# Feature weights of a Hedgehog attention kernel: two loads replaced by one load and a copy made by TensorE

## The chip, the cores and the metric

The kernel runs on one core of one Trainium2 chip. The metric is the time of one execution in device microseconds. The engines are TensorE (PE in the profile, with its weight loads as PEld), VectorE (DVE), ScalarE (ACT), GpSimd (POOL) and SyncE (SP, which here only issues DMAs).

## What is computed

Attention with a feature map instead of a softmax over keys, followed by a gated linear unit with a causal convolution of five taps, for 8 batches of 8 heads, 576 rows and 64 columns. Cut to what matters:

```
def phi(x):                                  # w_phi is 64 x 128
    proj = x @ w_phi
    proj = proj - max(|proj|, axis=-1)
    return concat([exp(proj), exp(-proj)])
q_p, k_p = phi(q), phi(k)
kv  = sum over s of k_p[s, f] * v[s, d]
z   = sum over s of k_p[s, f]
x   = (q_p @ kv) / (q_p @ z + 1e-6)          # heads side by side: 8 x 576 x 512
gate = sigmoid(causal 5-tap convolution of x with conv_w)
out  = (gate * (x @ w_val)) @ w_out
```

The weights `w_phi` are one 64 x 128 array of 32 KB, the same for q and k and for all heads and batches.

## The kernel before, in words

Each batch is laid out with two rows or two heads side by side: 64 columns of the one in partitions 0 to 63, of the other in partitions 64 to 127 (`par` 0 and 1 in the code). After a transpose, `XT_["k"]` and `XT_["q"]` (kT and qT in the profile) hold the inputs with the 64 columns over the partitions, in 18 blocks of 128 columns, worked on in five units (`UNITS`: 4, 4, 4, 4 and 2 blocks). For each block, `proj` (L570 to L578) runs two matmuls, one for each half of the partitions: the data stand in rows 0 to 63 or 64 to 127, and so the feature weights are needed in both halves too. That tile is `W2`, 128 x 128 in bf16, twice the same 64 rows. `qp` (L687) uses W2 the other way round, as the stationary operand.

`W2` is made in `c_w` (L451): ScalarE's queue issues two DMAs of `w_phi` into the two halves of `W32` (128 x 128, fp32), VectorE casts `W32` to `W2`, and ScalarE's queue then issues the load of the convolution weights `cw5`. (In the profile, buffer numbers are left out of names: W32 and W2 both appear as W.)

The first batch comes in by chunks: SyncE's queue issues four loads of K (`lk`, 288 KB each) and five of Q (`lq`, four of 256 KB and one of 128 KB) with `load32` (L520 to L527). They land in the memory of the second KTIL buffer, which is free at that time, so the profile shows them as KTIL. TensorE transposes them in fp32 (`tp32`, L536), and ScalarE or VectorE copies the result to bf16 (`tc32`, L542 and L544). Then come for each unit the K matmuls with W2 (`kp`), the row maxima on VectorE (`amax`, L585) and two exponentials on ScalarE (`kexp`, L595), and for Q the same with other steps between (`qm`, `mqt`, `rx`, `qp`, `qexp`). GpSimd waits for the last Q chunk (`hold`, L509) and then starts the loads of the next batches.

The order of the work is written out by hand. `build` makes a list of tasks, each with an index, an engine (or a choice of engines, settled by one letter of `FLEX`), and for tasks that write PSUM a group with one or two of the eight banks (digits of `BANKS`). `ORDER` lists the indices in the order in which the instructions are emitted; each engine runs its own instructions in that order. Durations and dependences given in `build` are notes for whoever made the order; the waits in the program follow from the tiles that are written and read. `WARM` and `ZERO` name positions in `ORDER` at which extra matmuls on constants are put in. A new task at the front of the list thus shifts every later index by one, and a new entry in `ORDER` every later position.

At the head, `ORDER` begins "1 2 9 3 4 11 5 6 10 21 22 19 20 13 12 46 ...": load K chunk 0, transpose K unit 0 (four transposes, bank 0), load K chunk 1, transpose K unit 1 (bank 3), load K chunk 2, copy unit 0 out, load Q chunks 1 and 0, transpose K unit 2 (bank 7), copy unit 1 out, K matmuls of unit 1, and so on. K unit 2 is the first that needs K chunk 2.

Of the kernel before, what the change touches and what calls it, by code (L numbers as in the profile page):

```python
# [17 lines left out]
F = 128  # L18
# [13 lines left out]
XH = R // 2  # L32
HALO = 16
XW = HALO + XH
WARM = (
    "60:6:1 81:1:1 87:7:2 134:7:1 141:7:1 "
)
ZERO = "35:76:7 61:80:5 75:34:1 101:105:1 118:99:1 126:215:8 144:223:1 155:192:4 158:200:1 175:315:6 189:346:1 195:241:2 197:241:2 211:327:1"
STD = 1.18
E1 = D + 1  # L40
QW = 2 * NR

ORDER = (
# [36 lines left out]
)  # L80
FLEX = (
    "AAAAAADAAADDPPPPDDDDAADDDDDDDDDDDDDAAADAAAADDDDAAADDDAADAAADDADAADDDDADDDDADDDDDDAADADDAAAAAA"
)
BANKS = (
    "037362307001454523232323016701676714232367230101676012354423010145454501013660564675601456745010145450101676767014501454"
    "545672012376701230167676745677773567232367232345452301672323232367674545015452343623670101232345454452230145450167676767"
    "010123014501230167450120167364012345236745454555723014545234567232323010123236745230167232346701422010167454567010121656"
    "701456701012301670123010167232367674567023677260123230123230167464644501016701670123676745672345232345450123670157672345"
    "010167452326322345670145670101674545012345012367452345010127452301014545670101765"
)  # L90


# [70 lines left out]
def build(plan, em=None):  # L163
# [16 lines left out]
    for b in range(B):  # L180

        if b == 0:
            last = A("lk", 0, 9, "SP", 0.3, None, rank=-1100)
            for w in "kq":
                lds = []
                for u in range(4 if w == "k" else NU):
                    pr = -1000.0 + (0 if w == "k" else 10) + u
                    last = A("l" + w, b, u, "SP", 0.65, fn("load32", w, u), [], rank=pr, lat=0.1)
                    lds.append(A("l" + w, b, u, "DMA", 0.9 if w == "k" else 0.2 * UNITS[u][1], None, [last], rank=pr))
                if w == "q":  # L190
                    hold = [None, A("lk", b, 0, "POOL", 0.15, fn("hold", HOLDU), [lds[HOLDU]], rank=-600)]
                for u, (c0, n) in enumerate(UNITS):
                    need = [lds[u]] if w == "q" else sorted(set(lds[J // 9] for J in (2 * c0, 2 * (c0 + n) - 1)), key=lambda t: t.idx)
                    pr = -900 + (0 if w == "k" else 50) + u
                    g = plan.group("tp", 1)
                    tp = A("kp", b, u, "PE", 0.22 * n, fn("tp32", w, u), need, g, 0, rank=pr)
                    h["x" + w, b, u] = A("kmax", b, u, ("DVE", "ACT"), (dve(n * P), act(n * P)), fn("tc32", w, u), [tp], g, rank=pr)
                    h["tp", w, u] = tp
# [62 lines left out]

        for u, (c0, n) in enumerate(UNITS):
            g = plan.group("kp", 2)
            kp = h["kp", b, u] = A("kp", b, u, "PE", 0.057 * n, fn("kp", b, u), [G("xk", b, u)], g, 1)
            h["kmax", b, u] = A("kmax", b, u, "DVE", dve(2 * n * P, 0.08), fn("kmax", b, u), [kp, G("ek", b - 2)], g)
            for s in range(2):
                h["kexp", b, u, s] = A("kexp", b, u, "ACT", act(2 * n * P), fn("kexp", b, u, s),
# [22 lines left out]

        for u, (c0, n) in enumerate(UNITS):
            g = plan.group("qm", 2)
            qm = h["qm", b, u] = A("qm", b, u, "PE", 0.057 * n, fn("qm", b, u), [G("xq", b, u)], g, 1)
            h["qmax", b, u] = A("qmax", b, u, "DVE", dve(2 * n * P, 0.08), fn("qmax", b, u), [qm, G("mqt", b - 2)], g)
        for i, us in enumerate(parts(b)):
            gm = plan.group("mqt", 1 if b == 0 else 2)
# [68 lines left out]
class Emit:  # L365
    def __init__(self, nc, tc, ctx, q, k, v, w_phi, moe_w_val, moe_conv_w, moe_w_out, out):
# [50 lines left out]
        ident = self.ident = T("ident", [P, P])  # L417
        nc.vector.tensor_copy(ident[:, :], ident_f[:, :])

        self.W32 = T("W32", [P, F], FP32)  # L420
        self.W2 = T("W2", [P, F])
        self.wphi = w_phi

# [26 lines left out]

    def c_w(self):  # L451
        nc = self.nc
        for i in range(2):
            nc.scalar.dma_start(self.W32[i * D:(i + 1) * D, :], self.wphi[:, :])
        nc.vector.tensor_copy(self.W2[:, :], self.W32[:, :])
        nc.scalar.dma_start(self.cw5[:, :], self.wts[1][:, :])

    def c_wv(self, t):
        self.nc.gpsimd.dma_start(self.WV[:, :, 0:DM], self.wts[0].rearrange("(i p) o -> p i o", p=P))
# [441 lines left out]
```

## Time and profile before

| what | value |
|---|---|
| median of three timed runs | 218.77 us (218.7, 218.77, 219.3) |
| span of the profiled execution, first to last instruction | 217.7 us |
| TensorE busy | 195.5 us, 90% of the span |
| ScalarE busy | 180.8 us, 83% |
| VectorE busy | 170.2 us, 78% |
| GpSimd busy | 132.8 us, 61% |
| data moved by DMA | 39.92 MB, 183 GB/s on the mean |

The profiled execution's own time is its span; what lies around the span is not in the trace. In lines of the profile, the name left of the arrow is written and the names right of it are read; the bracket at the end tells how long the engine had been idle and what ended that. In the chain of waits each line is a start, a duration and what was running or being waited for.

### The profile page before, as it was taken

What the parts mean: (1) busy time and instruction counts of PE and PEld (TensorE: products, weight loads), DVE (VectorE), ACT (ScalarE), POOL (GpSimd) and SP (SyncE); (2) the same over time, 40 slices, a digit from 0 to 9 for tenths busy, and PEclk for the clock granted to TensorE, in tenths of its full rate; (3) what the DMA queues carried; (4) which work ended last, traced back from release to release, by engine and by line L of the source; (5) the groups of instructions that cost most, each with busy time, mean ns of one, the idle gap of its engine ahead of it and who ended that gap; (6) DMA issues with size and microseconds to landing.
All of it is one profiled execution on the core that took longest, in us unless ns stands there. A gap on an engine that the chain in (4) does not pass through costs nothing.

```text
span 217.7 us, 9029 instructions
## 1 busy us (share of the span) xinstructions
PE 195.5 (90%) x3946; PEld 138.6 (64%) x3946; DVE 170.2 (78%) x257; ACT 180.8 (83%) x267; POOL 132.8 (61%) x172
## 2 busy tenths in 40 slices
PE   2787887778999999998999999999999999899990
PEld 2555565566676676676857776567757766687740
DVE  3199979999789988997899978998699897654510
ACT  3589999999989899998999997999988988634251
POOL 3055999897793838970999089902993879210010
PEclk9999999999999999999999999999999999999997
DMA  6999998899899799989999778969953265764166
GB/s 177 364 234 215 302 188 231 149 174 199 144 152 284 139 135 213 302 154 174 233 276 168 88 165 248 190 142 203 287 183 89 63 160 128 81 168 97 48 186 202
DMA packets 49954, 39.92 MB, mean 183 GB/s; under 512 B 34165, under 2 KB 39541, under 8 KB 49914
## 3 DMA queue, kind: packets, MB, share of 16 engines
q1 hardware_dynamic: 43616, 28.65, 55.6%
q0 software_dynamic: 6032, 10.49, 26.3%
q8 instruction: 31, 0.51, 0.9%
q10 hardware_dynamic: 266, 0.21, 0.3%
q14 instruction: 9, 0.07, 0.1%
HBM read 30.48 MB, written 9.44 MB: 183 GB/s over the span
## 4 chain that ended last, share of the span: by engine, by line
PE 52%; ACT 23%; DVE 14%; DMA 5%; issue 4%; SPq 0%; DVEq 0%; ACTq 0%
PE PS L791 11%; ACT QTIL L706 9%; PE PS L781 9%; PE PS L813 9%; ACT KTIL L595 8%; DVE MQP L585 5%; PE PS L620 5%; PE PS L577 4%; PE PS L719 4%; DVE MK L585 3%; DMA KTIL<-in_k_dram 3%; PE PS L693 2%; DMA XT<-XN 2%; PE PS L817 2%; PE PS L698 2%
## 5 line engine op out<-in xcount | busy, mean ns | idle before, releaser
L595 ACT ACTIVATE KTIL<-PS 128x1024 bf16<-128x1024 f32 (+1 forms) x80 | 71.9, 960 | 4.1 <-PE PS L577 2.0
L610 POOL TENSOR_TENSOR VT<-VN,EK 128x1152 bf16<-128x1152 f32 x32 | 67.9, 2123 | 4.0 <-ACT EK L604 3.9
L706 ACT ACTIVATE QTIL<-PS 128x1024 bf16<-128x1024 f32 x64 | 62.5, 1044 | 2.4 <-PE PS L698 1.6
L682 POOL TENSOR_TENSOR RX<-MQR,ident 128x512 bf16<-128x512 bf16 (+1 forms) x39 | 36.6, 964 | 35.7 <-DVE MQR L670 26.0
L585 DVE TENSOR_REDUCE MK<-PS 128x8 f32<-128x1024 f32 (+1 forms) x40 | 44.2, 1112 | 2.9 <-PE PS L577 1.2
L585 DVE TENSOR_REDUCE MQP<-PS 128x8 bf16<-128x1024 f32 (+1 forms) x40 | 43.6, 1112 | 3.1 <-PE PS L577 2.3
L791 PE MATMUL PS<-XT,WV 128*128 128x288 bf16 x256 | 34.8, 286 | 0.3 <-DVE GV L797 0.2
L797 DVE SCALAR_TENSOR_TENSOR GV<-TH,PS 128x576 bf16<-128x576 bf16 x32 | 23.8, 752 | 10.4 <-PE PS L791 4.7
L813 PE MATMUL PS<-WOUT,GV 128*128 128x512 bf16 x128 | 31.3, 380 | 0.0
L791 PEld LDWEIGHTS <-WV 128*128 128x128 bf16 x256 | 23.8, 98 | 7.9 <-issue 1.4
L785 ACT ACTIVATE TH<-PS 128x576 bf16<-128x576 f32 x32 | 20.3, 663 | 9.5 <-PE PS L781 6.3
L620 PE MATMUL PS<-VT,KTIL 64*128 64x65 bf16 x1152 | 23.3, 191 | 1.1 <-issue 1.0
L781 PE MATMUL PS<-XT,GW 64*64 64x288 bf16 x640 | 23.1, 285 | 0.9 <-DMA XT<-XN 0.8
L740 DVE TENSOR_TENSOR XN<-PS,RCP 128x512 bf16<-128x512 f32 x32 | 22.1, 692 | 1.5 <-DMA XT<-XN 0.4
L620 PEld LDWEIGHTS <-KTIL 64*128 64x128 bf16 x1152 | 20.8, 94 | 3.8 <-issue 2.5
L719 PEld LDWEIGHTS <-QTIL 128*128 128x128 bf16 x512 | 18.3, 97 | 6.4 <-issue 4.0
L719 PE MATMUL PS<-KV,QTIL 128*128 128x65 bf16 x512 | 20.3, 194 | 0.3 <-DVE MQP L585 0.2
L781 PEld LDWEIGHTS <-GW 64*64 64x64 bf16 x640 | 17.8, 106 | 3.3 <-DVE RCP L737 0.9
L634 ACT ACTIVATE OUTS<-PS 128x512 f32<-128x512 f32 x22 | 13.5, 619 | 7.3 <-PE PS L813 6.1
L577 PE MATMUL PS<-W,qT 64*128 64x128 bf16 x288 | 15.1, 217 | 3.7 <-ACT qT L544 0.9
L813 PEld LDWEIGHTS <-GV 128*128 128x128 bf16 x128 | 11.1, 98 | 11.3 <-issue 0.6
L577 PEld LDWEIGHTS <-qT 64*128 64x128 bf16 x288 | 10.6, 94 | 10.3 <-issue 5.2
(79 smaller groups left out, 235.6 us busy)
## 6 DMA issues: line engine op xcount, KB each, us to landing
out_dram<-OUTS SPq DMA_DIRECT2D x32, 256.0 KB, 3.4
VN<-in_v_dram SPq DMA_DIRECT2D x7, 1152.0 KB, 6.3
KQN<-in_q_dram POOLq DMA_DIRECT2D x6, 576.0 KB, 8.3
KQN<-in_k_dram POOLq DMA_DIRECT2D x6, 576.0 KB, 9.8
KTIL<-in_k_dram SPq DMA_DIRECT2D x4, 288.0 KB, 4.5
VN<-in_v_dram POOLq DMA_DIRECT2D x1, 1152.0 KB, 10.6
KTIL<-in_q_dram SPq DMA_DIRECT2D x4, 256.0 KB, 5.7
out_dram<-OUTS SPq DMA_DIRECT2D x14, 64.0 KB, 2.6
```

Of the source, the lines that this page charges most:

```text
L577: nc.tensor.matmul(self.PS[:, t.grp.banks[par], i * P:(i + 1) * P], X[rows, (c0 + i) * P:(c0 + i + 1) * P], self.W2[rows, :], start=True, ...
L585: self.nc.vector.tensor_reduce(o, self.two(t.grp, n * P).rearrange("p a (c f) -> p a c f", f=F), AX.X, ALU.max, apply_absolute_value=True)
L595: self.nc.scalar.activation(self.KTIL[b % 2][:, s, c0:c0 + n, :, :].rearrange("p c a f -> p a c f"), self.two(t.grp, n * P).rearrange("p a ...
L610: nc.gpsimd.tensor_tensor(self.VT[g][:, s, :, 0:D], self.VN[b % 2][:, NC * g:NC * g + NC, :], e.to_broadcast([P, NC, D]), ALU.mult)
L620: nc.tensor.matmul(self.PS[:, t.grp.banks[ab], (s * 2 + x) * E1:(s * 2 + x + 1) * E1], self.KTIL[b % 2][rows, s, J // 2, J % 2, :], self.V ...
L682: self.nc.gpsimd.tensor_tensor(o, *wide(self.MQR[self.mq(b, u)][:, :], self.ident2), ALU.mult)
L706: self.nc.scalar.activation(o, i, AF.Exp, scale=1.0 - 2.0 * s)
L719: nc.tensor.matmul(self.PS[:, t.grp.banks[h // 4], (h % 4) * E1:(h % 4 + 1) * E1], Q[:, s, c % 2, h, (c // 2) * P:(c // 2 + 1) * P], self. ...
L781: self.nc.tensor.matmul(self.PS[o * D:(o + 1) * D, t.grp.banks[par], 0:R], self.GW[r, jj, 4 - m, :], X[r, 4 * a + jj, :, HALO - 8 * s:HALO ...
L791: self.nc.tensor.matmul(self.PS[:, t.grp.banks[par], 0:R], self.WV[:, i, (2 * j + par) * D:(2 * j + par + 2) * D], X[:, 4 * par + i, :, HA ...
L797: nc.vector.scalar_tensor_tensor(out=self.GV[b % 3][:, j, :, :], in0=self.TH[j][:, :, :], scalar=1.0, in1=self.two(t.grp, R), op0=ALU.add, ...
L813: nc.tensor.matmul(self.PS[:, t.grp.banks[0], :], GV[:, j, c % 2, (c // 2) * XH:(c // 2) * XH + P], self.WOUT[:, j, c % 2, :], start=(j == ...
```

## The change

`w_phi` is loaded once, into a `W32` of 64 partitions, and cast by VectorE into a new bf16 tile `WB` of 64 partitions. Two new tasks stand at the front of the list. `c_wd`: TensorE multiplies a 64 x 64 identity with `WB`, twice, once into partitions 0 to 63 and once into partitions 64 to 127 of PSUM bank 7. `c_wd2`: VectorE copies the 128 x 128 result from PSUM into `W2`. A product with an identity in bf16 gives the bf16 values back, so W2 holds the same numbers as before. In `ORDER` the two stand behind the transposes of K unit 0 and ahead of the load of K chunk 1 and the transposes of K unit 1. All other entries of `ORDER` are in the same sequence, each index larger by two (index 0 stays); `FLEX` has one letter more at the front (D, for VectorE), `BANKS` one digit (7), and the positions and indices in `WARM` and `ZERO` are larger by two.

```
 ORDER = (
-    "1 2 9 3 4 11 5 6 10 21 22 19 20 13 12 46 25 26 7 8 23 24 14 27 28 42 29 ...
+    "3 4 11 1 2 5 6 13 7 8 12 23 24 21 22 15 14 48 27 28 9 10 25 26 16 29 30 44 31 ...
...
         if b == 0:
             last = A("lk", 0, 9, "SP", 0.3, None, rank=-1100)
+            g = plan.group("mqt", 1)
+            wd = A("mqt", 0, 0, "PE", 0.1, fn("c_wd"), [], g, 3, rank=-950)
+            h["w2",] = A("mqt", 0, 0, ("DVE", "ACT"), (dve(128), act(128)), fn("c_wd2"), [wd], g, rank=-950)
...
-        self.W32 = T("W32", [P, F], FP32)
+        self.W32 = T("W32", [D, F], FP32)
+        self.WB = T("WB", [D, F])
         self.W2 = T("W2", [P, F])
...
     def c_w(self):
         nc = self.nc
-        for i in range(2):
-            nc.scalar.dma_start(self.W32[i * D:(i + 1) * D, :], self.wphi[:, :])
-        nc.vector.tensor_copy(self.W2[:, :], self.W32[:, :])
+        nc.scalar.dma_start(self.W32[:, :], self.wphi[:, :])
+        nc.vector.tensor_copy(self.WB[:, :], self.W32[:, :])
         nc.scalar.dma_start(self.cw5[:, :], self.wts[1][:, :])
+
+    def c_wd(self, t):
+        for a in range(2):
+            self.nc.tensor.matmul(self.PS[a * D:(a + 1) * D, t.grp.banks[0], 0:F],
+                                  self.ident[0:D, 0:D], self.WB[:, :], start=True, stop=True)
+
+    def c_wd2(self, t):
+        self.ev(t, self.W2[:, :], self.PS[:, t.grp.banks[0], 0:F])
```

The first instructions of `kp` and `qm` for batch 0 also name the new copy as a dependence in `build`.

More of the change, by code (lines that the diff above doesn't have):

```diff
@@ L34 @@
 XW = HALO + XH
[L35 to L38, printed above, removed]
+WARM = "62:6:1 83:1:1 89:7:2 136:7:1 143:7:1"
+ZERO = "37:78:7 63:82:5 77:36:1 103:107:1 120:101:1 128:217:8 146:225:1 157:194:4 160:202:1 177:317:6 191:348:1 197:243:2 199:243:2 213:329:1"
 STD = 1.18
@@ L43 @@
 ORDER = (
[36 rows of a table removed]
[36 rows of a table added]
 )
 FLEX = (
-    "AAAAAADAAADDPPPPDDDDAADDDDDDDDDDDDDAAADAAAADDDDAAADDDAADAAADDADAADDDDADDDDADDDDDDAADADDAAAAAA"
+    "DAAAAAADAAADDPPPPDDDDAADDDDDDDDDDDDDAAADAAAADDDDAAADDDAADAAADDADAADDDDADDDDADDDDDDAADADDAAAAAA"
 )
 BANKS = (
[L85 to L89, printed above, removed]
+    "703736230700145452323232301670167671423236723010167601235442301014545450101366056467560145674501014545010167676701450145"
+    "454567201237670123016767674567777356723236723234545230167232323236767454501545234362367010123234545445223014545016767676"
+    "701012301450123016745012016736401234523674545455572301454523456723232301012323674523016723234670142201016745456701012165"
+    "670145670101230167012301016723236767456702367726012323012323016746464450101670167012367674567234523234545012367015767234"
+    "5010167452326322345670145670101674545012345012367452345010127452301014545670101765"
 )
@@ L263, in build @@
             g = plan.group("kp", 2)
-            kp = h["kp", b, u] = A("kp", b, u, "PE", 0.057 * n, fn("kp", b, u), [G("xk", b, u)], g, 1)
+            kp = h["kp", b, u] = A("kp", b, u, "PE", 0.057 * n, fn("kp", b, u), [G("xk", b, u), G("w2") if b == 0 else None], g, 1)
             h["kmax", b, u] = A("kmax", b, u, "DVE", dve(2 * n * P, 0.08), fn("kmax", b, u), [kp, G("ek", b - 2)], g)
@@ L292, in build @@
             g = plan.group("qm", 2)
-            qm = h["qm", b, u] = A("qm", b, u, "PE", 0.057 * n, fn("qm", b, u), [G("xq", b, u)], g, 1)
+            qm = h["qm", b, u] = A("qm", b, u, "PE", 0.057 * n, fn("qm", b, u), [G("xq", b, u), G("w2") if b == 0 else None], g, 1)
             h["qmax", b, u] = A("qmax", b, u, "DVE", dve(2 * n * P, 0.08), fn("qmax", b, u), [qm, G("mqt", b - 2)], g)
@@ L452, in c_w @@
         nc = self.nc
-        for i in range(2):
-            nc.scalar.dma_start(self.W32[i * D:(i + 1) * D, :], self.wphi[:, :])
-        nc.vector.tensor_copy(self.W2[:, :], self.W32[:, :])
+        nc.scalar.dma_start(self.W32[:, :], self.wphi[:, :])
+        nc.vector.tensor_copy(self.WB[:, :], self.W32[:, :])
         nc.scalar.dma_start(self.cw5[:, :], self.wts[1][:, :])
+    def c_wd(self, t):
+        for a in range(2):
+            self.nc.tensor.matmul(self.PS[a * D:(a + 1) * D, t.grp.banks[0], 0:F], self.ident[0:D, 0:D], self.WB[:, :], start=True, stop=True)
+    def c_wd2(self, t):
+        self.ev(t, self.W2[:, :], self.PS[:, t.grp.banks[0], 0:F])
     def c_wv(self, t):
```

72 rows, old and new, of the table ORDER are left out of this document.

## The prediction

> **What bounds the kernel now.** I read the page first, for the shares over the whole run, because the change touches only the first ten microseconds and I need to know whether a saving there is still there at the end.
>
> ```profile
> span 217.7 us, 9029 instructions
> PE 195.5 (90%) x3946; PEld 138.6 (64%) x3946; DVE 170.2 (78%) x257; ACT 180.8 (83%) x267; POOL 132.8 (61%) x172
> PE 52%; ACT 23%; DVE 14%; DMA 5%; issue 4%; SPq 0%; DVEq 0%; ACTq 0%
> ```
>
> No engine is free and none is full. The last row is the chain of waits that ended last: it hops between TensorE, ScalarE and VectorE, and only 5% of it is DMA. Every engine works through a written order, so a saving at the head of the chain can travel to the end, unless some other chain was nearly as late. So I read the chain in order of time for the head alone.
>
> ```profile
> 1.22 0.42 SPq L527
> 1.63 0.04 issue
> 1.67 5.58 DMA KTIL<-in_k_dram
> 7.25 0.04 issue
> 7.29 0.90 PE PS L536 x3
> 8.20 0.97 PE PS L577 x16
> 9.17 1.06 PE PS L536 x4
> ...
> 10.32 0.69 DVE qT L542
> 11.01 1.14 DVE MK L585
> ```
>
> The reader is to see that the third K chunk (issued at 1.67, landed at 7.25) is what the head waits for: three transposes of it, the first sixteen feature matmuls, four transposes of Q, and from 10.32 on VectorE and ScalarE hand on to each other. The feature weights W2, which the change is about, are not in the chain. So the question is what the change does to the landing at 7.25 and to TensorE between 3.85 and 10.3. That is the timeline's business, here by queue and engine (the row at 3.97 is the last of the three in the row above it):
>
> ```profile
> 0.73 1.23 ACTq L454 DMA_DIRECT2D W<-in_w_phi_dram  x2
> 0.74 1.37 SPq L527 DMA_DIRECT2D KTIL<-in_k_dram  x3
> 2.15 2.15 SPq L525 DMA_DIRECT2D KTIL<-in_q_dram  x3
> 3.97 0.33 SPq L525 DMA_DIRECT2D KTIL<-in_q_dram  x1
> 3.85 2.23 PE L536 MATMUL PS<-ident_f,KTIL 128*128 128x128 f32 x9 [3.85 <-DMA KTIL<-in_k_dram]
> 7.29 0.90 PE L536 MATMUL PS<-ident_f,KTIL 128*128 128x128 f32 x3 [1.21 <-DMA KTIL<-in_k_dram]
> 8.13 1.04 PE L577 MATMUL PS<-W,kT 64*128 64x128 bf16 x16
> ...
> 11.07 0.40 PE L577 MATMUL PS<-W,qT 64*128 64x128 bf16 x8 [0.19 <-DVE qT L542]
> ...
> 20.95 0.61 PE L555 MATMUL PS<-ident,QTIL 128*128 128x128 bf16 x8
> 5.29 0.23 DVE L455 CAST W<-W 128x128 bf16<-128x128 f32 x1 [2.48 <-DMA W<-in_w_phi_dram]
> 10.32 0.69 DVE L542 CAST qT<-PS 128x512 bf16<-128x512 f32 x1 [4.80 <-ACT KTIL L595]
> ...
> 16.69 0.21 DVE L667 TENSOR_SCALAR MQR<-PS 128x128 bf16<-128x128 bf16 x1
> 11.01 0.19 POOL L509 CAST HOLD<-KTIL 128x1 bf16<-128x1 f32 x1 [8.62 <-DMA KTIL<-in_q_dram]
> ```
>
> Three covers show. TensorE ends its first nine transposes at 6.08 and stands idle for 1.21 us until the third K chunk. W2 is cast by 5.52 and first used at 8.13, so it has 2.6 us in hand. VectorE is idle for 4.80 us before 10.32. Next the DMAs at the head, by issue with its time to landing (the first four rows are K chunks 0, 1 and 2 and the second W copy), with the two waits of SyncE's queue, the share of the ScalarE queue between 1.70 and 7.25, and the DMA share (next-to-last column, then GB/s) in two stretches.
>
> ```profile
> KTIL<-in_k_dram SPq DMA_DIRECT2D x1, 288.0 KB, 3.0
> KTIL<-in_k_dram SPq DMA_DIRECT2D x1, 288.0 KB, 3.5
> KTIL<-in_k_dram SPq DMA_DIRECT2D x1, 288.0 KB, 5.6
> W<-in_w_phi_dram ACTq DMA_DIRECT2D x1, 32.0 KB, 3.8
> KTIL<-in_q_dram SPq DMA_DIRECT2D x1, 256.0 KB, 5.7
> SPq L525 <- DMA W<-in_w_phi_dram: 1.2, 2, 0.8
> q10 hardware_dynamic: 170, 0.08, 4.8%
> 2.70:3.70 1.00, 0.00 (x0) 0.00 (x0) 0.11 (x2) 0.94 (x1) 0.00 (x0) 1.00 1.05 392
> 4.20:4.70 0.50, 0.50 (x4) 0.34 (x2) 0.00 (x0) 0.00 (x0) 0.00 (x0) 1.00 0.72 201
> ```
>
> Chunk 0 lands at 0.74 + 3.0 = 3.7, chunk 1 at 1.22 + 3.5 = 4.7, chunk 2 at 7.25, the second W copy at 1.35 + 3.8 = 5.15 (its issue is the second half of the 1.23 us row). At 2.70 to 3.70 the engines are full (share 1.05, 392 GB/s); at 4.20 to 4.70 there is a dip to 201 GB/s in the middle of chunk 2's flight. The first W copy has no landing time in the trace, but the Q issue at 3.97 is one of the two that waited for W, so that copy had landed by about 3.95.
>
> **The change part by part.** *One W copy fewer.* ScalarE issues one W load instead of two, and the conv weights behind it go out about 0.6 us earlier, which nothing in the head reads. What the lost copy takes from the DMA engines ahead of chunk 2 I bound from two rows. From below: ScalarE's queue, two W copies and the conv weights, took 4.8% of 16 engines over 5.55 us, which is 0.27 us of each engine; one copy is under half of it, 0.12. From above: 288 KB is 0.295 MB, at 392 GB/s 0.75 us, but chunk 1 landed 1.0 us after chunk 0, with the first W copy between them; if all of the excess is that copy, it costs 0.25. Less than nothing is also possible: where engines idle anyway, as in the dip, the copy's packets cost 0. I take 0.2, between the two rows and near the upper one, because the landing is what the path sees. Chunk 2 then lands at about 7.05, and that comes off the chain.
>
> The Trainium skill, "DMA: Bandwidth & Descriptors", Rules for kernel authors, says that two transfers to disjoint partition halves serialize on the same engines and that one should be used instead. The rows agree so far as the copies take engine time one after the other; by the 436 GB/s of its Anatomy section the copy's 32 KB would be an estimated 0.08 us, which would give 218.7 instead of 218.6.
>
> *SyncE's queue.* The two Q issues that waited for W (1.2 us together, 0.8 the longer) read no W. I take this to be a completion counter that an earlier DMA still holds, each issue reusing the counter of one a fixed number before it. With one DMA fewer at the front, the Q issue at 3.97 goes out up to 0.8 us earlier and those behind it 0.4 to 0.8. It buys nothing on the path: they queue behind chunk 2 and the first two Q chunks (the first of these lands at 2.15 + 5.7 = 7.85, and its transposes start at 9.17, 1.3 us later). The last Q chunk releases POOL at 11.01, which then loads the next batch; that may start 0.2 to 0.4 us earlier, and TensorE first touches the next batch at 20.95.
>
> *The cast.* 64 rows instead of 128, 0.23 us by the row, at about 4.05 instead of 5.29, since it waits for the first copy only: done by 4.3.
>
> *Two matmuls on TensorE, between the first four transposes and the next five.* By the nine in 2.23 us, 0.23 us each, the first four are issued by about 4.75, so the cast at 4.3 is not waited for. Sixteen W matmuls in 1.04 us run in pairs, 0.13 us a pair; the two new ones share their rows of the array, so I count a pair's time for each: 0.26 us. The next five transposes end at 6.34 instead of 6.08, and still 0.7 us ahead of 7.05: cost nothing, cover the wait for chunk 2. If that cover goes, 0.26 us goes onto the chain. Queued behind the new wait are all of TensorE's later transposes; who waits for those is ScalarE's copies, which have the same slack.
>
> *The copy out of PSUM on VectorE.* 128x128 from PSUM: the nearest row is 0.21 us (L667). It runs at about 5.4 to 5.6, inside VectorE's 4.80 us of idle time; W2 is ready at 5.6 instead of 5.52, needed at 7.9. It uses PSUM bank 7, which the third transpose group writes next; the group's first transpose may be held to 5.6, behind which it stands anyway. Cost nothing.
>
> The sum: 217.7 of span less 0.2 is 217.5. The three timed runs have a median of 218.77, 1.07 above the profiled span, and I take that difference as unchanged: 217.5 + 1.07 = 218.57, so 218.6. About 0.3%, or 0.66 us, is what a measurement of this kernel can tell from no change (its own runs spread from 218.7 to 219.3), so the forecast is "no difference that shows". From 10.3 us on I assume that the whole 0.2 travels. If another chain takes over, less does: 218.8. With the two bounds and half a run's spread, its own range is 218.3 to 219.0.
>
> **The rivals.** *The dip goes with the copy.* Chunk 2 lands 2.55 us after chunk 1 where 0.75 would do. If the small packets from ScalarE's queue cause that hold-up, chunk 2 lands a microsecond or more earlier. TensorE then becomes the bound at 6.34 (five transposes behind the new pair), and the gain is 7.25 - 6.34, or 0.9: 217.9. For it: the dip falls in the W copies' flight. Against it: one W copy flew beside chunk 1, which came in at nearly full rate.
>
> *The weights come late.* TensorE's queue is in order, so a late W load now holds all K transposes, where it formerly held only the first W matmuls at 8.13. It decides if W lands after about 5.4: then 0.1 + 0.23 for the cast, 0.26 for the pair and five transposes at 0.23 reach beyond 7.1, and each further microsecond is lost one for one. At 6.4 it is 1.0 us: 219.8. Against it: the first copy had landed by 3.95 and even the second at 5.15.
>
> *The TensorE clock turns earlier.* The matmuls tell of it: W matmuls run sixteen in 1.04 us at 8.13 and eight in 0.40 at 11.07.
>
> ```profile
> L536 PE MATMUL PS<-ident_f,KTIL 128*128 128x128 f32 x16 | 4.2, 433 | 5.1 <-DMA KTIL<-in_k_dram 5.1
> L536 PE MATMUL PS<-ident_f,KTIL 128*128 128x128 f32 x19 | 3.3, 295 | 0.3 <-DVE MQP L585 0.3
> ```
>
> The same transposes take 433 ns on the mean before 10 us and 295 after 10.6, although the granted clock of the windows reads 1.00 in both. If the two new matmuls shorten the idle time enough to bring the turn forward to 7.3, the 2.9 us of TensorE work in the chain from 7.29 to 10.2 shrinks by the ratio of the means, to 2.0: 0.9 us, plus the 0.2: 217.7. The Trainium skill, "TensorE: Matmul & The Clock Gate", Part 1, says that the clock rises after a busy window of about 3.4 us which runs free of the kernel; the same rule would let an unlucky phase delay the turn as easily, and no row of one execution can show either. Against it: 0.26 us of work in a 1.21 us hole leaves most of the hole.
>
> *The change brings nothing*: the copy's packets filled time in which the engines waited, and chunk 2 lands at 7.25 as before: 218.8.
>
> **How the numbers follow.** Forecast 0.60, nothing at all 0.16, dip gone 0.13, clock earlier 0.04, weights late 0.07. The predicted time is the forecast's, 218.6. The range runs from 217.8, which takes in the dip gone, to 219.1, which takes in the spread of no gain at all and leaves out the late weights. Faster by over 0.3% means under 218.11: dip and clock, 0.17, and 0.02 of the forecast's lower tail. Slower by over 0.3% means above 219.43: late weights, 0.07. The same: 0.74.
>
> **What would show it.** Right: one W row on ScalarE's queue; the cast before 4.75; two small matmuls between the fourth and fifth transpose; the five transposes done by 6.4 and then idle time ended by the third K chunk at 7.0 to 7.2; the chain of waits still opening with that chunk. Wrong: idle time on TensorE ended by the cast or by W; the third K chunk at 6.3 or earlier, or later than 7.4; transposes at 295 ns before 10 us; a span outside 216.7 to 218.0.

## The result, and the profile after

The kernel after takes 217.94 us in the median of 22 runs, the kernel before 218.8 us in 22 runs beside them. The ratio is 0.994 with a 95% interval of 0.9918 to 0.9961: faster, by 0.4 to 0.8%. Ratios leave out executions in a slower state of the chip and the medians do not, so the two medians are only 0.86 us apart where the ratio says 1.3. The forecast was 218.6 and "no difference that shows"; the range began at 217.8, so it held the median, but the direction was called wrong.

The page of the kernel after, in the same three rows as before:

```profile
span 215.2 us, 9031 instructions
PE 195.4 (91%) x3948; PEld 138.4 (64%) x3948; DVE 170.0 (79%) x258; ACT 180.5 (84%) x267; POOL 132.9 (62%) x172
PE 55%; ACT 22%; DVE 15%; issue 4%; DMA 1%; DVEq 0%; ACTq 0%
```

The engines' work is the same; the DMA share of the chain of waits fell from 5% to 1%. Of that, the K chunks went from 3% to 1%; the other 2% (a transfer named XT<-XN, later in the run) is missing from a second profile of the kernel before too (below, "before, twice"), so it is not the change's. The chain's head tells where the K chunks' part went (start, duration, what):

```profile
0.74 2.93 DMA KTIL<-in_k_dram
3.66 0.14 issue
3.80 1.09 PE PS L544 x4
4.89 0.24 PE PS L461 x2
5.13 1.90 PE PS L544 x8
7.03 0.97 PE PS L585 x16
8.00 0.71 PE PS L544 x4
...
8.80 0.69 DVE qT L550
```

The chain no longer waits for the third K chunk. After the first chunk TensorE runs through without a pause: four transposes, the two new doubling matmuls, eight transposes, the W matmuls. VectorE's first Q copy starts at 8.80 instead of 10.32, 1.52 us earlier. The timeline has the parts of the change (queues, TensorE, VectorE):

```profile
0.73 0.58 ACTq L455 DMA_DIRECT2D W<-in_w_phi_dram  x1
2.14 1.38 SPq L533 DMA_DIRECT2D KTIL<-in_q_dram  x3
4.82 0.31 PE L461 MATMUL PS<-WB,ident 64*64 64x128 bf16 x2
5.06 1.97 PE L544 MATMUL PS<-ident_f,KTIL 128*128 128x128 f32 x8
6.96 1.04 PE L585 MATMUL PS<-W,kT 64*128 64x128 bf16 x16
3.98 0.22 DVE L456 CAST WB<-W 64x128 bf16<-64x128 f32 x1 [1.58 <-DMA W<-in_w_phi_dram]
5.17 0.29 DVE L636 CAST W<-PS 128x128 bf16<-128x128 f32 x1 [0.97 <-PE PS L461]
```

And the landing of the third K chunk, issued at 1.67, stands in the DMA issues (the last number is the time from issue to landing):

```profile
KTIL<-in_k_dram SPq DMA_DIRECT2D x1, 288.0 KB, 4.1
```

It takes 4.1 us instead of 5.6: it lands at 5.81, while TensorE is still on the second unit's transposes. The W matmuls start at 6.96 instead of 8.13 (1.17 us), and from there to the Q copy it takes 1.84 us instead of 2.19 (0.35 us), because the last four transposes of the chain ran in 0.71 us instead of 1.06: the clock had turned. (By that is meant here that TensorE works slowly at first and from some moment on faster: the sixteen W matmuls take 1.04 us in both kernels, and 0.62 in those below that are warmed up.)

The two profiled spans differ by 2.5 us, the medians by 0.9. The head makes 1.52 us of the 2.5. The rest, 1.0 us, is about the length of a pause that nothing in the profile releases. The chain of the kernel before has it at 98 us:

```profile
98.03 0.96 issue
```

A second profile of the same kernel (below, "before, twice") has it at half the length,

```profile
98.23 0.47 issue
```

and the profile of after has none there. A second profile of after (e16 below), however, has two:

```profile
91.36 0.83 issue
96.85 0.70 issue
```

So these pauses vary between executions of one kernel and are not the change's; what makes them is not shown.

One more thing is earlier in after: GpSimd's wait for the last Q chunk ends at 9.95 us instead of 11.01, and its loads of the next batches with it. That this is not the source of the gain is told by the warmed kernel of before (e7 below), which gains as much with that wait ending at 10.68:

```profile
9.95 0.19 POOL L517 CAST HOLD<-KTIL 128x1 bf16<-128x1 f32 x1 [7.41 <-DMA KTIL<-in_q_dram]
10.68 0.19 POOL L509 CAST HOLD<-KTIL 128x1 bf16<-128x1 f32 x1 [8.29 <-DMA KTIL<-in_q_dram]
```

### The profile page after: what moved, and what is told of

Its sections match the earlier page's. It is cut to its first block, busy times and chain, and to the rows that moved or that the text cites. A ratio compares the mean times of both kernels' runs of the same rounds, so it can differ in the third digit from the quotient of the medians.

```text
span 215.2 us, 9031 instructions
## 1 busy us (share of the span) xinstructions
PE 195.4 (91%) x3948; PEld 138.4 (64%) x3948; DVE 170.0 (79%) x258; ACT 180.5 (84%) x267; POOL 132.9 (62%) x172
## 4 chain that ended last, share of the span: by engine, by line
PE 55%; ACT 22%; DVE 15%; issue 4%; DMA 1%; DVEq 0%; ACTq 0%
PE PS L799 11%; PE PS L821 10%; PE PS L789 9%; ACT QTIL L714 9%; ACT KTIL L603 9%; DVE MQP L593 5%; PE PS L727 5%; PE PS L585 4%; PE PS L628 4%; DVE MK L593 4%; PE PS L701 2%; PE PS L825 2%; PE PS L706 2%; PE PS L544 2%; DVE XN L748 2%
## 5 line engine op out<-in xcount | busy, mean ns | idle before, releaser
L789 PE MATMUL PS<-XT,GW 64*64 64x288 bf16 x640 | 23.6, 285 | 0.9 <-DVE RCP L745 0.4
```

What stands on the lines that cost most here:

```text
L789: self.nc.tensor.matmul(self.PS[o * D:(o + 1) * D, t.grp.banks[par], 0:R], self.GW[r, jj, 4 - m, :], X[r, 4 * a + jj, :, HALO - 8 * s:HALO ...
```

## The experiments

Three theories at first. A: the second copy's own rows, ahead of the third K chunk, hold that chunk up. B: the conv weights do, which the change moves ahead of the chunk. C: the landing varies by itself, and the gain has another source. Later D: a share of the gain is TensorE's clock.

**The copy put back, idle (e1, e15).** The kernel after, and the second load again, into a tile that nothing reads:

```
+        nc.scalar.dma_start(self.WX[:, :], self.wphi[:, :])      # behind the load of W32, [D, F] fp32
```

> The kernel after, with a second load of the feature weights put back in its old place on ScalarE's queue, into a tile that nothing reads. Theory A (the second copy's own packets and its place ahead of the third K chunk hold that chunk up): the third K chunk lands at 6.8 to 7.3 us as before and the time is 218.6 to 219.0, no better than the kernel before. Theory B (the conv weights do it: the change moves them ahead of that chunk): the same here, since the idle copy pushes them back too. Theory C (the landing varies by itself from one execution to the next, and the gain has another source): the time stays near 217.9.

The ratio to before is 1.0003 (0.9971 to 1.0036). TensorE's timeline of this kernel:

```profile
4.90 0.31 PE L463 MATMUL PS<-WB,ident 64*64 64x128 bf16 x2
5.15 1.33 PE L546 MATMUL PS<-ident_f,KTIL 128*128 128x128 f32 x5
6.86 0.90 PE L546 MATMUL PS<-ident_f,KTIL 128*128 128x128 f32 x3 [0.38 <-DMA KTIL<-in_k_dram]
7.69 1.03 PE L587 MATMUL PS<-W,kT 64*128 64x128 bf16 x16
```

The wait for the third chunk is back (landing at 6.81), and the whole gain is gone, though TensorE still doubles the weights. Theory C falls, and the doubling by itself brings nothing. Once more, on another occasion:

> The kernel with the idle second copy of the feature weights once more, on the same chip as the two with other sources: 6.4 to 7.2 us for the third K chunk and the time of before, by all theories.

1.004 (1.000 to 1.008), landing at 7.02.

**The copy behind the chunk (e2).** The kernel before, with no work added to TensorE:

```
-        for i in range(2):
-            nc.scalar.dma_start(self.W32[i * D:(i + 1) * D, :], self.wphi[:, :])
-        nc.vector.tensor_copy(self.W2[:, :], self.W32[:, :])
+        nc.scalar.dma_start(self.W32[0:D, :], self.wphi[:, :])
...
+            if u == 2:                                            # in load32, behind K chunk 2
+                self.nc.sync.dma_start(self.W32[D:P, :], self.wphi[:, :])
+                self.nc.vector.tensor_copy(self.W2[:, :], self.W32[:, :])
```

> The kernel before, with the second copy of the feature weights issued by SyncE's queue right behind the third K chunk, so that the conv weights go out second on ScalarE's queue; nothing is added on TensorE. Theories A and B: the third K chunk lands at 5.8 to 6.1 us, and without the 0.24 us of the two new matmuls the time is 217.6 to 217.9, at least as good as after. Theory C: 218.8, as before.

0.991 (0.9875 to 0.9946), landing at 5.50. Its timeline on TensorE:

```profile
3.90 2.79 PE L537 MATMUL PS<-ident_f,KTIL 128*128 128x128 f32 x12 [3.90 <-DMA KTIL<-in_k_dram]
6.63 1.03 PE L578 MATMUL PS<-W,kT 64*128 64x128 bf16 x16
7.59 1.35 PE L537 MATMUL PS<-ident_f,KTIL 128*128 128x128 f32 x8
```

All twelve K transposes run in one piece. The gain is had without the doubling and without one DMA fewer: what counts is that the copy is not ahead of the chunk.

**The conv weights late (e3), and before, twice (e4).** The kernel before with the conv weights issued by SyncE behind the last Q chunk; and the kernel before, unchanged.

```
-        nc.scalar.dma_start(self.cw5[:, :], self.wts[1][:, :])
+            if u == 4:                                            # in load32, behind Q chunk 4
+                self.nc.sync.dma_start(self.cw5[:, :], self.wts[1][:, :])
```

> The kernel before, both weight copies in place, with the conv weights moved from ScalarE's queue to SyncE's, behind the last Q chunk. Theory A: the third K chunk still lands at 6.8 to 7.3 us and the time stays 218.6 to 219.0. Theory B: it lands at 5.8 to 6.1 us and the time is 217.7 to 218.0. Theory C: 218.8, landing anywhere.

> The kernel before, unchanged, timed and profiled once more. Theories A and B: the third K chunk lands at 6.8 to 7.3 us again and TensorE's clock turns at its own moment. Theory C: the landing differs by half a microsecond or more from the 7.25 us of the first profile. Time 218.8 by all.

e3: 0.9969 (0.9935 to 1.0002), landing at 6.41, between the two expectations and unclear in time. e4: 0.9994 (0.997 to 1.0017), landing at 6.83. So the landing does vary from one execution to the next, as C said (by 0.4 us here, and by 1.1 between the two profiles of one kernel below, e10 and e14), but around a later moment than in after.

**One row, two copies, the copy last (e5, e6, e11).** The kernel after with idle loads of other sizes and places on ScalarE's queue:

```
+        nc.scalar.dma_start(self.WX[0:1, :], self.wphi[0:1, :])   # e5: one row, behind W32
+        nc.scalar.dma_start(self.WX[:, 0, :], self.wphi[:, :])    # e6: two copies, behind W32
+        nc.scalar.dma_start(self.WX[:, 1, :], self.wphi[:, :])
+        nc.scalar.dma_start(self.WX[:, :], self.wphi[:, :])       # e11: one copy, behind the conv weights
```

> The kernel after with an idle extra load in the old place of the second copy, but of one row of 512 bytes instead of 64 rows. Theory A1 (what holds the third K chunk up is the rows of the extra load, spread over all DMA engines): it lands near 5.8 us, as in after. Theory A2 (it is the extra load as such, its issue and completion, whatever its size, and the conv weights pushed behind the chunk): it lands at 6.4 to 7.2 us, as with the full idle copy.

> The kernel after with two idle extra loads of the feature weights instead of one, between the weights and the conv weights on ScalarE's queue. Theory A1 (rows) and A2 (each load): the third K chunk lands later still than with one (6.81 us), at 7.2 to 7.9. If the hold-up comes from the conv weights' place alone, behind the chunk's issue, it lands at 6.4 to 7.2, as with one.

> The kernel after with the idle second load of the feature weights behind the conv weights on ScalarE's queue, so that it is issued at about 2.1 us, after the third K chunk (1.67). If only what is issued ahead of the chunk holds it up, it lands at 5.6 to 6.0 us; if anything on that queue at that time does, at 6.3 to 7.2 us.

Landings: 5.79 with one row, 6.66 with two copies, 5.45 with the copy last. With one row the conv weights are issued at 2.07, behind the chunk, and it lands as in after: theory B falls, and so does a cost of each DMA as such. The two copies do not add up; but the second was issued at 1.99, behind the chunk, and e11 shows that what is issued there does not hold it up, so this was no double dose.

**The other queue (e9).** The idle copy on SyncE's queue, between the second and third K chunk.

```
+            if u == 1:                                            # in load32, behind K chunk 1
+                self.nc.sync.dma_start(self.WX[:, :], self.wphi[:, :])
```

> The kernel after with an idle second load of the feature weights, 64 rows, issued by SyncE's queue between the second and the third K chunk instead of by ScalarE's. If rows of an extra load hold the third K chunk up wherever they come from, it lands at 6.3 to 7.2 us; if it is the second queue's rows between those of the K chunks that do it, it lands at 5.9 to 6.2 us, later than in after by the copy's own engine time and its issue alone.

Landing at 6.66; but the chunk itself was issued at 2.31 instead of 1.67 and took 4.4 us, against 3.8 to 4.1 without a copy. Most of the delay is the later issue, so this does not tell the two readings apart.

**Another source (e10, e13, e14).** 64 rows of 512 bytes from other arrays in the copy's old place:

```
+        nc.scalar.dma_start(self.WX[:, :], self.wts[0][0:D, 0:F])                    # e10, e14: value weights
+        nc.scalar.dma_start(self.WX[:, :], self.src["v"][7].rearrange("h t d -> (h t d)")
+                            .rearrange("(p x) -> p x", x=F)[0:D, :])                 # e13: V, contiguous
```

> The kernel after with an idle extra load of 64 rows of 512 bytes in the old place on ScalarE's queue, but read from another array (a corner of the value weights). If the hold-up comes from reading the same 32 KB twice, the third K chunk lands near 5.8 us; if from rows of any source, at 6.4 to 7.2 us as with the idle copy.

> The kernel after with an idle extra load of 64 rows of 512 bytes in the old place of the second copy, read as one contiguous stretch of another input (the last batch of V). If reading the same 32 KB a second time is what costs, the third K chunk lands at 5.5 to 6.1 us and the time is within 0.3% of after (0.992 to 0.997 of before); if 64 rows of any source cost, at 6.4 to 7.2 us and the time is that of before.

> The kernel with the idle load from the value weights once more, now timed. If the source matters, the third K chunk lands below 6.3 us again and the time is 0.992 to 0.997 of before; if the first landing at 6.15 us was one early execution, it lands at 6.4 to 7.2 and the time is that of before.

e10 landed at 6.15, early for a held-up chunk, so the same kernel was timed as e14. e13: 6.09, and 1.0037 (0.9985 to 1.009). By that landing e13 is within what was expected if only the same 32 KB cost (5.5 to 6.1), by its time it is like before. Its profiled execution has a head nearly as early as that of after (Q copy at 8.96) and loses the gain later: TensorE pauses for 1.93 us at 47.6 us without a releaser, and the granted clock (third number from the end) falls to 0.71 between 50 and 55 us, where it reads 1.00 in after.

```profile
47.58 1.93 issue
50.00:55.00 5.00, 4.70 (x75) 3.36 (x71) 3.85 (x7) 2.42 (x3) 1.67 (x3) 0.71 1.06 202
```

So one profile tells of one execution, and the verdict goes by the times. e14, the kernel of e10 once more, took the longest of all,

```profile
KTIL<-in_k_dram SPq DMA_DIRECT2D x1, 288.0 KB, 5.6
```

landing at 7.28, and 1.0025 (0.9989 to 1.0061). The time is that of before with either source: reading the same 32 KB twice is not the cause.

**After, again (e16).**

> The kernel after, unchanged, once more: the third K chunk lands at 5.4 to 5.9 us, TensorE does not pause between its first transposes and the W matmuls, and the time is 0.992 to 0.996 of before.

0.9968 (0.9928 to 1.0008), landing at 5.53, no pause on TensorE. This interval reaches past 1, but overlaps the first one.

**The clock (e7, e8, e12).** Five matmuls on constants in front of the first transposes, by an entry "2:1:5" in `WARM`: e7 is the kernel before with them, e8 the kernel of e2, e12 the kernel after.

> The kernel before, with five matmuls on constants put in front of TensorE's first transposes, where it stands idle; all DMAs as in before. Theory D (part of the gain is TensorE's clock, which turns to full some 3.4 to 6 us after TensorE stops pausing): the clock turns between 4.9 and 8.3 us although the third K chunk still lands at 6.8 to 7.3, the work between that landing and VectorE's first Q copy takes 1.6 to 2.2 us instead of 3.0, and the time is 217.5 to 218.2. If the clock has no part: 218.8, and the copy at 10.3 as before.

> The kernel before, with the second weight copy behind the third K chunk on SyncE's queue and the same five matmuls in front. Theories A and D together: the third K chunk lands at 5.5 to 5.8 us, the clock turns between 4.9 and 8.3, VectorE's first Q copy starts at 7.2 to 8.5, and the time is 216.4 to 217.3, below after. If the two gains are one and the same: no better than 217.4.

> The kernel after, with the five matmuls on constants in front of the first transposes. If the clock's share of the head is what the other warmed kernels say, VectorE's first Q copy starts at 8.1 to 8.5 us and the time is 216.6 to 217.3, a little above the warmed kernel with the late copy because the two doubling matmuls stand in the chain. If the doubling matmuls cost nothing, it equals that kernel (216.6).

e7: 0.9915 (0.9876 to 0.9955), with all DMAs as in before and the chunk landing at 6.97. TensorE's timeline:

```profile
1.46 2.31 PE L491 MATMUL PS<-ONES 128*128 128x512 bf16 x5 [1.46 <-DVE ONES L396]
3.89 1.66 PE L536 MATMUL PS<-ident_f,KTIL 128*128 128x128 f32 x9
7.02 0.55 PE L536 MATMUL PS<-ident_f,KTIL 128*128 128x128 f32 x3 [1.47 <-DMA KTIL<-in_k_dram]
7.50 0.62 PE L577 MATMUL PS<-W,kT 64*128 64x128 bf16 x16
8.05 1.09 PE L536 MATMUL PS<-ident_f,KTIL 128*128 128x128 f32 x8
```

The wait for the chunk is as long as ever, but sixteen W matmuls take 0.62 us instead of 1.04 and the eight transposes 1.09 instead of 1.78. The clock, moved forward, gives as much as the whole change (the chunk's landing, 0.28 us earlier than in the first profile of before, is within what that kernel varies by). e8: 0.9882 (0.9858 to 0.9906); both gains in one, its timeline:

```profile
3.89 2.79 PE L537 MATMUL PS<-ident_f,KTIL 128*128 128x128 f32 x12
6.61 0.62 PE L578 MATMUL PS<-W,kT 64*128 64x128 bf16 x16
```

Its Q copy starts at 7.93. (The profiled execution itself took 219.24 us, with a pause of 2.43 us at 95 us; only its head is read here.) This is the fastest version here, 1.2% below before, and its interval ends below that of the change. e12: 0.9928 (0.9881 to 0.9974), Q copy at 7.88. Whether the doubling costs anything against e8 the intervals do not say.

All heads side by side, in us (landing of the third K chunk, start of the W matmuls, start of the first Q copy):

| kernel | 64 further rows issued ahead of the chunk | landing | W matmuls | Q copy | ratio to before |
|---|---|---|---|---|---|
| before | yes | 7.25 | 8.13 | 10.32 | |
| e4 before, twice | yes | 6.83 | 7.71 | 9.89 | 0.9994 |
| e3 conv weights late | yes | 6.41 | 7.29 | 9.47 | 0.9969 |
| e1, e15 idle copy | yes | 6.81, 7.02 | 7.69, 7.89 | 9.88, 10.09 | 1.0003, 1.004 |
| e6 two idle copies | yes | 6.66 | 7.54 | 9.73 | one run, 219.98 us |
| e9 idle copy, SyncE's queue | yes, chunk issued 0.64 later | 6.66 | 7.54 | 9.35 | one run, 218.36 us |
| e10, e14 value weights | yes | 6.15, 7.28 | 7.06, 8.16 | 8.97, 10.35 | one run, 217.79 us; 1.0025 |
| e13 V | yes | 6.09 | 6.99 | 8.96 | 1.0037 |
| after, e16 | no | 5.81, 5.53 | 6.96, 7.18 | 8.80, 8.92 | 0.994, 0.9968 |
| e5 one row | one row | 5.79 | 6.95 | 9.01 | one run, 218.10 us |
| e11 idle copy last | no | 5.45 | 7.13 | 9.32 | one run, 218.67 us |
| e2 copy behind the chunk | no | 5.50 | 6.63 | 8.61 | 0.991 |
| e7 before, warmed | yes | 6.97 | 7.50 | 8.81 | 0.9915 |
| e8 copy behind, warmed | no | 5.50 | 6.61 | 7.93 | 0.9882 |
| e12 after, warmed | no | 5.48 | 6.56 | 7.88 | 0.9928 |

Eleven executions with 64 further rows ahead land at 6.09 to 7.28, with 6.81 in the middle; seven without at 5.45 to 5.81, with 5.50 in the middle. The two groups do not overlap, and the middles are 1.3 us apart. The gap between them, 0.28 us, is smaller than what one kernel varies by (e10, e14), so no single landing proves much; but the times agree: the four series with an idle copy ahead (e1, e13, e14, e15) have 1.0003 to 1.004, the three without any and not warmed (after, e16, e2) 0.991 to 0.9968. Only the interval of e16 (0.9928 to 1.0008) meets those of the first four.

From the W matmuls to the Q copy it takes 2.18 to 2.20 us in the eight executions that pause for the chunk and are not warmed, but for e9 (1.81); 1.74 to 2.06 in those that go through, but for e11 (2.19); and 1.31 to 1.32 in the warmed three. So the clock turns earlier where there is no pause, as a rule and not always.

## Why the prediction was wrong, by its own steps

**The step that failed** is the price of the lost copy: "I take 0.2, between the two rows and near the upper one". It was 1.44 us in the pair of profiles (7.25 to 5.81) and some 0.3 to 1.8 over all of them, with bounds of 0.12 and 0.25. Both bounds were of the wrong kind. The lower counted the time of the copy's packets, the upper looked at the pair of K chunks around the first copy. The row that had the answer was on the page: the third chunk took 5.6 us where the first took 3.0, and 0.75 us of engine time does not explain the 2.55 us between the landings. The text used that row for a rival, "the dip goes with the copy", and gave it 0.13.

**That rival is what happened on the path:** the chunk lands before TensorE is ready for it, TensorE becomes the bound with the pair in its queue, and the gain is TensorE's wait. Two things in it are not as it said. Its time, 217.9, is the measured median by some luck: it comes from a gain of 0.9 us, and the head gained 1.52 (1.17 of it TensorE's wait, the rest the clock), the ratio of the times 1.3. And the dip that it named is still there in the profile of after, 242 GB/s where before had 201 (in the second profile of after it is 365); what went is the late landing.

```profile
4.20:4.70 0.50, 0.50 (x4) 0.28 (x2) 0.00 (x1) 0.00 (x0) 0.00 (x0) 1.00 0.87 242
```

Two of the prediction's signs of being wrong came true with it: the chunk landed before 6.3, and the span was below 216.7. The argument against that rival, that one W copy flew beside chunk 1 without harm, is true of after as well (chunk 1 lands at 4.5 to 4.8 us in every profile that tells, with a copy ahead of the third chunk or not); it does not carry over to the next 64 rows, and the runs do not say why.

**The clock** was a rival of its own, with 0.04. It is not an alternative but mostly comes with the other: when the chunk is early, TensorE does not pause, and the clock tends to turn while it works through. It gave 0.35 us of the 1.52. The prediction looked for what the two new matmuls fill of the pause, and not at the pause closing from the other end. The Trainium skill, "TensorE: Matmul & The Clock Gate", Part 1, has the clock rise after about 3.4 us of busy time, in a window that runs free of the kernel. The warmed kernels do not contradict it: their first matmul starts at 1.46, and their transposes or W matmuls run at the faster rate from about 4.9 (e7), 5.2 (e12) and 6.6 us (e8) on, 3.4 to 5.1 us later.

**Right, with small errors:** the cast at 3.98 in 0.22 us (foreseen 4.05), the pair 0.24 us on TensorE (0.26), the wait for the cast hidden, the copy out of PSUM 0.29 us (0.21) in idle time of VectorE. The cover of the pair is gone, as foreseen for that rival: it is in the chain. SyncE's third Q issue goes out 0.9 us earlier, and only one issue waits for W, now of a K chunk:

```profile
SPq L535 <- DMA W<-in_w_phi_dram: 0.4, 1, 0.4
```

That fits the reading of a counter reused by a later DMA, which no run here shows, and no time on the path hangs on it. The Trainium skill's rule on two transfers to disjoint halves ("DMA: Bandwidth & Descriptors", Rules for kernel authors) pointed the right way; the estimate from the page's rate, 0.08 us, was further off than the rows (the Anatomy section gives that rate for DMAs issued by GpSimd). The whole gain of the head was still there at 30 us: the maxima on VectorE that before starts at 31.70 start 1.51 us earlier:

```profile
30.19 1.13 DVE MK L593
```

## What to carry to other kernels

A small load costs what it delays, not the time of its own packets: where a large transfer that the chain waits for takes far longer than its bytes, look at what was issued ahead of it, and move that behind. Read the excess of a landing over its bytes as a size of possible gain before pricing the part that is removed. And a pause on TensorE early in a kernel is paid twice, once as the wait and once as work at the low clock behind it; idle time before the first data can be used to turn the clock.

## What the runs showed of the hardware

- 64 rows of 512 bytes issued on ScalarE's queue just ahead of a 288 KB load on SyncE's queue went with a landing of that load at 6.09 to 7.28 us (ten executions), against 5.45 to 5.81 us in the seven without, whatever array they came from. One row did not hold it up (one execution), and 64 rows issued behind it did not (three). Between 4.0 and 4.5 us the DMA engines moved 410 GB/s in e2 and 161 in e15:

```profile
4.00:4.50 0.50, 0.50 (x3) 0.50 (x4) 0.00 (x0) 0.00 (x0) 0.00 (x0) 1.00 1.06 410
```

```profile
4.00:4.50 0.50, 0.50 (x3) 0.50 (x4) 0.22 (x1) 0.04 (x1) 0.00 (x0) 1.00 0.90 161
```

- That rate is no sure sign (after itself moved 230 there and its chunk was early). Why the rows cost so much more than their packets stays open. In the packet records of the traces the longest K packet (2304 bytes) that starts after 3.5 us and before the landing took 0.85 to 1.50 us in the kernels with rows ahead, and at most 0.84 us in the others, where the middle packet takes 0.09; what holds such a packet is not shown.
- The granted clock reads 1.00 in the windows before 10 us, while sixteen W matmuls take 1.04 us there in before and 0.62 in the warmed kernels: the clock at the start is told by durations alone.
- In e2 TensorE's work up to 6.6 us was fp32 transposes only, and of its eight Q transposes (7.59, 1.35 us; 1.97 in e11, 1.09 warmed) a part already ran at the faster rate, about 4.4 us after the first transpose and 1.7 after the first W matmul. That suggests that transposes count as busy time for the clock; it was not tried alone. The delay is not a fixed one: in e11, which goes through without a pause from 3.96 us on just the same, all eight Q transposes still took the slow rate's 1.97 us, up to 10.06.
